# Gated linear attention and a gated feed-forward on one core: all five engine orders laid out anew

## The chip, the core and the metric

The kernel runs on one core of a Trainium2 chip. A core has five engines that run their own instruction lists side by side: TensorE (PE, matrix multiplies; the loads of its stationary operand stand as PEld), VectorE (DVE), ScalarE (ACT), GpSimd (POOL) and SyncE (SP, which here only issues DMAs). ACT and POOL issue DMAs too, each on a queue of its own. The engines wait for each other through semaphores. TensorE writes into eight PSUM banks, which VectorE and ScalarE empty. The metric is the device time of one execution in microseconds (us), lower is better.

## The reference

The first half is a gated linear attention over 4 batches, 8 heads, 768 tokens and 48 channels. The second half is a feed-forward block over the 3072 rows of the first one's result.

```python
f = 1.0 / (1.0 + np.exp(-f_logit))
for t in range(S):
    state = f[:, :, t, :, None] * state + np.einsum('bhd,bhe->bhde', k[:, :, t], v[:, :, t])
    y[:, :, t] = np.einsum('bhd,bhde->bhe', q[:, :, t], state)
...
gate = np.maximum(x @ w_gate, 0.0)      # x: (3072, 384), w_gate and w_val: (384, 1536)
val = x @ w_val
return (gate * val @ w_out)             # w_out: (1536, 384)
```

## The kernel before, in words

**Attention.** The recurrence is done in chunks of 128 tokens (6 chunks of 4 batches, 24 steps). For a step, ScalarE turns `f` into the logarithm of the gate (Exp, then Ln, lines 484 and 487, 768 columns for two steps at once). TensorE sums it along the tokens with a triangular matrix (names beginning with `cum`, lines 503 to 517), ScalarE takes Exp of the sum with both signs (lines 528 and 530) and of the chunk's total decay (line 538). VectorE or GpSimd multiply `q` and `k` with these (the "hats", names `hq` and `hk`, lines 552 on GpSimd and 553 on VectorE). The hats are transposed, on TensorE for the first eight steps (names `tq`, `tk`, line 564, and a copy to SBUF, names `cq`, `ck`, lines 568 and 569) and by a DMA for the others. Scores follow (`s`, lines 596 and 662), a mask on VectorE (`m`, lines 604 and 669), the result inside the chunk (`y`, lines 684 and 757), the part that comes from the state (`yi`, line 720) and the new state (`kv`, lines 707 and 784).

**Units.** The first eight steps are done as four units of two steps: unit 0 has the steps 00 and 01, unit 1 the steps 02 and 03, then 10 and 11, then 12 and 13 (a name such as `hk02` is the `k` hat of step 02). A unit works with pieces of the array: 64 matmuls of 64x32 for a `y`, 32 of 48x64 for its scores, 16 of 64x128 for a `kv`. Each of them is one matmul instruction and one weight load, so such a step issues many short instructions. These are the "tiled steps" below, with the scores (`s`) and the results (`y`) of later chunks that also use a part of the array.

**Feed-forward.** For a group of four steps (512 rows) and each of 12 blocks of 128 hidden columns, TensorE makes a gate (`g`) and a value (`u`), three matmuls each (line 804). ScalarE or VectorE applies the maximum with zero (`r`, lines 809 and 810), and VectorE multiplies (`p`, line 812). The first group's blocks 0 to 3 are done for two steps at a time (256 columns). The output projection (`o`, line 825) takes 12 matmuls a step, a copy (`d`) and a store. After some 20 us the feed-forward's matmuls fill TensorE between the attention's steps.

**What sets the order.** Nothing is scheduled at run time. A table `ORDER` lists, for each engine, the numbers of its operations in order; `BANKS` gives the PSUM bank of each result in the order in which TensorE opens them; `HELD` adds waits: `48: 10` lets operation 48 wait for operation 10. A negative number in TensorE's list stands for fill, matmuls on zeros (line 889) whose results are not used: `~3512` is three of 512 columns. Whoever opens a bank waits until its last tenant has been read. Semaphore waits follow from the data and these banks.

**Loads.** At the start each unit needs four transfers of 384 KB (`f`, `k`, `q`, `v`), written f0.0, k0.0 and so on for unit 0, f0.2 and so on for unit 1, f1.0 for the third, f1.2 for the fourth. They go over SP's queue, one (q0.0) over ScalarE's. The weights go over GpSimd's queue, in pieces.

## Time and profile before

| what | value |
|---|---|
| median of 3 runs | 193.1 us (192.79 to 193.47) |
| the profiled execution | 193.01 us, of it the span 191.3 us |
| TensorE busy | 180.6 us (94% of the span) |
| VectorE, ScalarE, GpSimd busy | 137.4 us, 92.0 us, 59.2 us |
| granted TensorE clock | 1.0 in all slices |

The span is the time from the first to the last instruction; 1.7 us of the profiled execution lie around it. A busy TensorE is not one at its peak, since matmuls overlap and their ends are modelled. So pauses are read from the starts of neighbouring instructions, and from the chain of work that ended last, which is followed back from the last instruction. "Issue" in a chain or a wait is time for which the profile names no reason. A name in a row such as L804 is the line of the kernel before; the lines of the changed kernel are one higher from the table on.

### The profile page before, as it was taken

The numbers are of one execution on the slowest core, as the hardware profiler recorded it, in microseconds if no ns is written. First come the engines' busy times: TensorE is split into PE (matmuls) and PEld (weight loads), VectorE is DVE, ScalarE is ACT, GpSimd is POOL, SyncE is SP. The second block draws the span as 40 slices with busy tenths as digits, with TensorE's granted clock in tenths as the row PEclk, the third lists the DMA queues.
The fourth block names the chain that finished last, engine by engine and source line by source line (L and its number), as shares of the span: only waits on it lengthen the run. The fifth ranks groups of instructions, "written<-read, shape, count | busy, mean of one in ns | idle before, by whom it ended". The sixth has DMA issues, their size and how long they took to land.

```text
span 191.3 us, 4793 instructions
## 1 busy us (share of the span) xinstructions
PE 180.6 (94%) x1977; PEld 108.4 (57%) x1996; DVE 137.4 (72%) x249; ACT 92.0 (48%) x200; POOL 59.2 (31%) x88
## 2 busy tenths in 40 slices
PE   7597999989899999999999999999999999999994
PEld 7364785455655556655555654556656554455562
DVE  4299877986758778669868779988688485655620
ACT  3969663264477546497654574372233132301112
POOL 5638531741036702047371610492600000000000
PEclk9999999999999999999999999999999999999999
DMA  6999999969999999989999999999763300000223
GB/s 163 318 296 216 159 209 264 161 123 251 225 221 206 240 201 246 235 191 200 197 182 215 245 175 175 243 251 178 98 151 108 99 4 0 3 0 0 109 98 126
DMA packets 110278, 32.43 MB, mean 170 GB/s; under 512 B 103472, under 2 KB 110000, under 8 KB 110256
## 3 DMA queue, kind: packets, MB, share of 16 engines
q1 hardware_dynamic: 88960, 25.04, 61.7%
q0 software_dynamic: 3744, 3.54, 12.2%
q10 hardware_dynamic: 17552, 3.54, 10.0%
q8 instruction: 16, 0.26, 0.6%
q14 instruction: 6, 0.05, 0.1%
HBM read 25.95 MB, written 4.72 MB: 160 GB/s over the span
## 4 chain that ended last, share of the span: by engine, by line
PE 85%; DVE 8%; DMA 3%; issue 2%; ACT 0%; DVEq 0%; ACTq 0%
PE ps L804 46%; PE ps L825 25%; DVE hats L553 4%; DMA q_in<-in_q_dram 3%; PE ps L596 2%; PE ps L757 2%; PE ps L564 2%; PE ps L514 1%; DVE gT L812 1%; PE ps L662 1%; PE ps L684 1%; PE ps L784 1%; DVE ptm L669 1%; PE ps L768 1%; PE ps L764 1%
## 5 line engine op out<-in xcount | busy, mean ns | idle before, releaser
L812 DVE TENSOR_TENSOR gT<-relu,ps 128x512 bf16<-128x512 bf16 (+1 forms) x76 | 47.7, 653 | 19.7 <-PE ps L804 17.5
L804 PE MATMUL ps<-xT,wv 128*128 128x512 bf16 (+1 forms) x220 | 53.6, 367 | 0.6 <-issue 0.2
L804 PE MATMUL ps<-xT,wg 128*128 128x512 bf16 (+1 forms) x219 | 52.6, 368 | 0.6
L825 PE MATMUL ps<-wo,gT 128*128 128x384 bf16 (+2 forms) x300 | 52.0, 320 | 0.0
L809 ACT ACTIVATE relu<-ps 128x512 bf16<-128x512 f32 (+1 forms) x42 | 23.9, 576 | 47.8 <-PE ps L804 24.2
L825 PEld LDWEIGHTS ps<-wo,gT 128*128 128x128 bf16 x300 | 27.7, 98 | 18.3
L804 PEld LDWEIGHTS ps<-xT,wg 128*128 128x128 bf16 x228 | 23.6, 108 | 20.5 <-issue 0.4
L804 PEld LDWEIGHTS ps<-xT,wv 128*128 128x128 bf16 x228 | 23.3, 108 | 18.3
L552 POOL TENSOR_TENSOR hats<-q_in,expo 128x384 bf16<-128x384 f32 x17 | 17.9, 1058 | 30.2 <-DMA q_in<-in_q_dram 12.2
L810 DVE TENSOR_SCALAR relu<-ps 128x512 bf16<-128x512 f32 (+1 forms) x34 | 21.7, 654 | 5.4 <-PE ps L804 5.3
L552 POOL TENSOR_TENSOR hats<-k_in,expo 128x384 bf16<-128x384 f32 x17 | 17.7, 1050 | 21.2 <-ACT expo L528 14.9
L604 DVE TENSOR_TENSOR ptm<-ps,tri 128x512 bf16<-128x512 f32 x32 | 20.5, 684 | 5.1 <-PE ps L596 5.1
L831 ACT ACTIVATE osb<-ps 128x384 f32<-128x384 f32 (+1 forms) x16 | 7.6, 484 | 25.0 <-PE ps L825 22.2
L528 ACT ACTIVATE expo<-ps 128x384 f32<-128x384 f32 x24 | 11.7, 496 | 6.1 <-DVE hats L553 2.6
L530 ACT ACTIVATE expo<-ps 128x384 f32<-128x384 f32 x24 | 11.8, 492 | 2.0 <-PE ps L517 1.9
L460 POOL TENSOR_TENSOR st<-ssum,dec 128x384 bf16<-128x384 f32 x10 | 8.6, 864 | 10.0 <-DVE ssum L458 10.0
L669 DVE TENSOR_TENSOR ptm<-ps,tmask 128x512 bf16<-128x512 f32 x16 | 10.0, 678 | 2.1 <-PE ps L662 2.1
L484 ACT ACTIVATE f_in<-f_in 128x768 f32<-128x768 f32 x12 | 10.1, 840 | 2.8 <-DMA f_in<-in_f_logit_dram 2.8
L458 DVE TENSOR_TENSOR ssum<-ps,st 128x384 f32<-128x384 f32 x16 | 8.8, 550 | 2.7 <-PE ps L784 2.5
L553 DVE TENSOR_TENSOR hats<-q_in,expo 128x384 bf16<-128x384 f32 x7 | 8.2, 1167 | 3.4 <-DMA q_in<-in_q_dram 3.4
L487 ACT ACTIVATE bneg<-f_in 128x768 bf16<-128x768 f32 x12 | 10.1, 841 | 1.0 <-ACT osb L831 0.8
L564 PE MATMUL ps<-ident,hats 128*128 128x128 bf16 x64 | 5.5, 220 | 4.0 <-DVE hats L553 3.0
(78 smaller groups left out, 159.2 us busy)
## 6 DMA issues: line engine op xcount, KB each, us to landing
v_in<-in_v_dram SPq DMA_DIRECT2D x12, 384.0 KB, 5.5
out_dram<-osb SPq DMA_DIRECT2D x23, 192.0 KB, 2.3
k_in<-in_k_dram SPq DMA_DIRECT2D x10, 384.0 KB, 7.1
q_in<-in_q_dram SPq DMA_DIRECT2D x9, 384.0 KB, 5.8
f_in<-in_f_logit_dram SPq DMA_DIRECT2D x8, 384.0 KB, 4.8
f_in<-in_f_logit_dram ACTq DMA_DIRECT2D x4, 384.0 KB, 6.6
q_in<-in_q_dram ACTq DMA_DIRECT2D x3, 384.0 KB, 5.6
wv<-in_moe_w_val_dram POOLq DMA_DIRECT2D x2, 384.0 KB, 6.7
```

The source lines that it names most:

```text
L484: add(f"ef{c}{b0}", by("ACT", lambda: sc.activation(raw, raw, AF.Exp, scale=-1.0), act_(n)), keys, keys, key=P)
L528: add(f"ek{c}{b}", by("ACT", lambda: sc.activation(ex[:, 1, :], bc.ap[:, 0:HD], AF.Exp, scale=1.0), act_(HD)), [bc], [f"expk{ei}"], key=P + 1)
L530: add(f"eq{c}{b}", by("ACT", lambda: sc.activation(ex[:, 0, :], bc.ap[:, 0:HD], AF.Exp, scale=-1.0), act_(HD)), [bc], [f"expq{ei}"], key=P ...
L552: return {**by("POOL", lambda: gp.tensor_tensor(o, i_, e_, ALU.mult), pool_(HD)), **by("DVE", lambda: ve.tensor_tensor(o, i_, e_, ALU.mult ...
L553: **by("DVE", lambda: ve.tensor_tensor(o, i_, e_, ALU.mult), dve_(HD))}
L604: add(f"m{c}{b}{j}", by("DVE", lambda b=b, j=j, mi=mi: ve.tensor_tensor(ptm[mi][:, j, :, :], s[b, j].ap[:, :].rearrange("p (n t) -> p n t" ...
L669: add(f"m{c}{b2[i]}{j}", by("DVE", lambda i=i, j=j, mask=mask: ve.tensor_tensor(ptm[mi[i]][:, j, :, :], s[j, i].ap[:, :].rearrange("p (n t ...
L804: z = te.matmul(bank.ap[:, 0:n], wt[:, kt, w_cols(j)], xT[xi][:, kt, n0:n1], start=(kt == 0), stop=(kt == NK - 1))
L809: add(f"r{c}{b0}.{j}", {**by("ACT", lambda: sc.activation(rdst, gate.ap[:, 0:n], AF.Relu), act_(n)), **by("DVE", lambda: ve.tensor_scalar_ ...
L810: **by("DVE", lambda: ve.tensor_scalar_max(rdst, gate.ap[:, 0:n], 0.0), dve_(n))}, [gate], [f"relu{ri}"], key=P)
L812: add(f"p{c}{b0}.{j}", by("DVE", lambda: ve.tensor_tensor(gT[gi][:, j, n0:n1], rdst, val.ap[:, 0:n], ALU.mult), dve_(n)), [val, f"relu{ri} ...
L825: z = te.matmul(o.ap[:, 0:e1 - e0], gT[gi][:, j, b * C:(b + 1) * C], wo[:, j, e0:e1], start=(j == 0), stop=(j == NJ - 1))
```

## The change

All numbers of the three tables change; the code below them stays. The operations are the same, but for the fill. Of the diff two lines of each kind tell it:

```diff
 ORDER = {
     "PE": [
-        45, ~60100, 74, 85, ~3512, 82, ~3512, 90, 80, 92, 121, ~1512, 95, 110, 101, 126, ~4512, 116, ~2512, 100, 128,
+        45, ~12512, 85, 74, ~9512, 110, 90, 121, 92, 82, 80, ~1512, 101, 95, 116, ~1512, 137, 126, 128, 118, 100, 104,
...
     "ACT": [
-        48, 72, 73, 108, 76, 75, 86, 87, 109, 84, 91, 122, 123, 111, 120, 127, 112, 77, 117, 113, 264, 103, 265, 228,
+        47, 49, 72, 73, 108, 76, 86, 75, 109, 87, 77, 113, 111, 122, 91, 93, 120, 123, 112, 130, 264, 117, 127, 129,
...
 HELD = {
-    48: 10, 57: 114, 60: 140, 67: 284, 69: 164, 70: 185,
+    47: 25, 56: 77,
 }
...
 BANKS = [
-    0, 1, 2, 3, 4, 5, 6, 7, 1, 2, 3, 4, 5, 6, 7, 1, 3, 7, 0, 2, 1, 4, 5, 6, 3, 0, 2, 7, 1, 5, 2, 0, 1, 3, 6, 0, 2, 3,
+    0, 1, 2, 3, 4, 5, 6, 7, 0, 1, 3, 7, 6, 5, 4, 0, 2, 6, 5, 7, 4, 6, 3, 0, 5, 7, 1, 4, 6, 0, 3, 4, 7, 6, 2, 5, 6, 7,
```

The fill goes from 60 matmuls of 100 columns and 13 of 512 to 24 of 512. Of the holds, those on q1.0 (60, after `yi03`), v1.2 (67), the weight loads wv2+2 (57), wv8+4 (69) and wo0+4 (70) go. New are one on k0.0 (47, after a memset of GpSimd) and one on the weight load wg2+2 (56), which now waits for ScalarE's decay of unit 0 (77, `dc00`). The places below are those that the prediction speaks of.

**The first loads.** SP's queue before, from its first row (f0.0 and f0.2, then k0.0, v0.0, k0.2, v0.2, q0.2, f1.2 and f1.0; q0.0 is ScalarE's first DMA):

```order
L408 DMA f_in<-in_f_logit_dram 128x8x96 x2
L408 DMA k_in<-in_k_dram 128x8x96
L408 DMA v_in<-in_v_dram 128x8x96
L408 DMA k_in<-in_k_dram 128x8x96
L408 DMA v_in<-in_v_dram 128x8x96
L408 DMA q_in<-in_q_dram 128x8x96
L408 DMA f_in<-in_f_logit_dram 128x8x96 x2
L408 DMA q_in<-in_q_dram 128x8x96 x2
```

SP's queue in the changed kernel, from the same place:

```order
L409 DMA f_in<-in_f_logit_dram 128x8x96 x2
L409 DMA q_in<-in_q_dram 128x8x96
L409 DMA k_in<-in_k_dram 128x8x96
L409 DMA v_in<-in_v_dram 128x8x96
L409 DMA q_in<-in_q_dram 128x8x96
L409 DMA f_in<-in_f_logit_dram 128x8x96 x2
L409 DMA q_in<-in_q_dram 128x8x96
L409 DMA k_in<-in_k_dram 128x8x96 x2
```

The q of unit 0 has come over to SP's queue, and k0.0 and v0.0 have gone to ScalarE's, where they are its first two instructions; what follows on SP stands one place further ahead.

**ScalarE around the Exp of f1.2.** Before, from the Exps of step 02 on (`expo<-ps4`; lines 528 and 530). The row of line 484 is the Exp of f1.2, the first row of line 487 its Ln; `qkT` are the copies of the transposes, `xT0<-ps3` is the first row block for the feed-forward:

```order
L528 ACTIVATE expo<-ps4 128x384
L584 ACTIVATE vpad2<-v_in 128x4x2x48
L569 ACTIVATE qkT<-ps7 128x512
L530 ACTIVATE expo<-ps4 128x384
L538 ACTIVATE dec<-ps0 64x4x2 x2
L569 ACTIVATE qkT<-ps1 128x512
L538 ACTIVATE dec<-ps4 64x4x2 x2
L484 ACTIVATE f_in<-f_in 128x768
L609 ACTIVATE xT0<-ps3 128x3x2x64
L487 ACTIVATE bneg<-f_in 128x16x48
```

In the changed kernel, from the last `v` copy of unit 1 on:

```order
L585 ACTIVATE vpad3<-v_in 128x4x2x48
L485 ACTIVATE f_in<-f_in 128x768
L570 ACTIVATE qkT<-ps4 128x512
L570 ACTIVATE qkT<-ps6 128x512
L570 ACTIVATE qkT<-ps5 128x512
L488 ACTIVATE bneg<-f_in 128x16x48
L610 ACTIVATE xT0<-ps4 128x3x2x64
L485 ACTIVATE f_in<-f_in 128x768
L488 ACTIVATE bneg<-f_in 128x16x48
```

The Exp of f1.2 now stands ahead of three copies of unit 1's transposes; before it stood behind the last of ScalarE's.

**VectorE in the first feed-forward group.** Before, from the last two 512-column maxima ahead of the first `hq` (step 11) to the end of the group's products:

```order
L810 TENSOR_SCALAR relu<-ps 128x512 x2
L812 TENSOR_TENSOR gT<-relu,ps 128x512 x2
L553 TENSOR_TENSOR hats<-q_in,expo 128x8x48
L812 TENSOR_TENSOR gT<-relu,ps 128x512 x2
L553 TENSOR_TENSOR hats<-k_in,expo 128x8x48
L810 TENSOR_SCALAR relu<-ps 128x512 x2
L553 TENSOR_TENSOR hats<-k_in,expo 128x8x48
L812 TENSOR_TENSOR gT<-relu,ps 128x512
L568 COPY qkT<-ps 128x512
L812 TENSOR_TENSOR gT<-relu,ps 128x512
```

In the changed kernel, from the hat of k for step 13 on:

```order
L554 TENSOR_TENSOR hats<-k_in,expo 128x8x48
L813 TENSOR_TENSOR gT<-relu,ps 128x512
L330 MEMSET dec 128x32
L813 TENSOR_TENSOR gT<-relu,ps 128x512
L811 TENSOR_SCALAR relu<-ps 128x512
L813 TENSOR_TENSOR gT<-relu,ps 128x512
L554 TENSOR_TENSOR hats<-q_in,expo 128x8x48
L813 TENSOR_TENSOR gT<-relu,ps 128x512
L569 COPY qkT<-ps 128x512
L811 TENSOR_SCALAR relu<-ps 128x512
L813 TENSOR_TENSOR gT<-relu,ps 128x512
L569 COPY qkT<-ps 128x512
```

Two hats stand among the 512-column operations where three stood (a hat of q, step 10, has moved ahead of them, between 256-column ones), and two copies of transposes are new there.

**TensorE's tiled steps of units 2 and 3.** Before, from the second scores on (line 662 scores, 707 `kv`, 684 `y`, 720 `yi`, 825 output projection, 514 and 517 sums):

```order
L662 MATMUL ps<-qkT 64x128 x32
L825 MATMUL ps<-wo,gT 128x384 x12
L707 MATMUL ps<-vpad,hats 128x96 x32
L684 MATMUL ps<-ptm,vpad 32x128 x128
L720 MATMUL ps<-qkT,st_0 32x128 x24
L514 MATMUL ps<-bneg,tri 128x384
L517 MATMUL ps<-ones,bneg 128x1 x4
L825 MATMUL ps<-wo,gT 128x384 x4
```

In the changed kernel, from the same scores on:

```order
L663 MATMUL ps<-qkT 64x128 x32
L826 MATMUL ps<-wo,gT 128x384 x12
L685 MATMUL ps<-ptm,vpad 32x128 x64
L708 MATMUL ps<-vpad,hats 128x96 x32
L826 MATMUL ps<-wo,gT 128x384 x8
L515 MATMUL ps<-bneg,tri 128x384
L518 MATMUL ps<-ones,bneg 128x1 x4
L826 MATMUL ps<-wo,gT 128x384 x4
L721 MATMUL ps<-qkT,st_0 32x128 x12
L685 MATMUL ps<-ptm,vpad 32x128 x64
L721 MATMUL ps<-qkT,st_0 32x128 x12
```

The two `y` steps, 64 matmuls each, stood back to back; now 12 matmuls of the output projection and a sum stand between them.

1 line of the change is left out of this document (added), and 98 rows, old and new, of tables (BANKS, ORDER).

## The prediction

> **What bounds the kernel now.** I read the page first, then the windows, TensorE's waits, the chain and, around each break in it, the timeline.
>
> ```profile
> PE 180.6 (94%) x1977; PEld 108.4 (57%) x1996; DVE 137.4 (72%) x249; ACT 92.0 (48%) x200; POOL 59.2 (31%) x88
> ...
> GB/s 163 318 296 216 159 209 264 161 123 251 225 221 206 240 201 246 235 191 200 197 182 215 245 175 175 243 251 178 98 151 108 99 4 0 3 0 0 109 98 126
> ...
> q8 instruction: 16, 0.26, 0.6%
> ```
> ```profile
> 76.34:81.20 4.86, 4.86 (x128) 3.27 (x128) 3.05 (x6) 2.33 (x9) 0.00 (x0) 1.00 1.27 234
> ```
>
> The first row holds busy time and instructions of each engine, the second the bytes moved in 40 slices of 4.8 us, the third the transfers of instructions. In the window's row the first column after its length is TensorE's busy time, with the count of matmuls: it is busy for the whole 4.86 us. The chain too runs along TensorE almost alone after the tiled steps of the first 60 us. So TensorE is the bound there, and since the change leaves its work as it is, time can only be won or lost in the first 60 us, at the end, and where TensorE changes its form of work. The chain names the places (start, length, work):
>
> ```profile
> 22.98 0.66 PE ps L684 x62
> ...
> 33.31 2.09 DVE hats L553
> 35.45 0.40 PE ps L564 x4
> ...
> 38.85 1.28 DVE hats L553
> 40.12 0.61 DVE gT L812
> 40.78 0.62 PE ps L564 x8
> ...
> 50.91 0.58 PE ps L684 x54
> 51.50 0.55 issue
> ...
> 167.16 0.65 PE ps L825 x4
> ```
>
> Three things are to be seen. Up to unit 1's `y` at 22.98 the start-up runs at the pace of loads, ScalarE and VectorE. Between 33 and 41 us VectorE's hats carry the chain. And at 51.5 us TensorE pauses inside a `y` step, after 54 of its 64 matmuls, where no semaphore is waited for.
>
> **The start.** In the changed kernel I follow ScalarE from the landing F of f1.2, since the Exp of f1.2 now stands ahead of three copies that unit 1 needs:
>
> ```profile
> 14.80 0.36 ACT L538 ACTIVATE dec<-ps 64x8 f32<-64x8 f32 x2
> ...
> 16.27 0.84 ACT L484 ACTIVATE f_in<-f_in 128x768 f32<-128x768 f32 x1
> 17.14 0.60 ACT L609 ACTIVATE xT<-ps 128x384 bf16<-128x384 f32 x1
> 17.60 0.82 ACT L487 ACTIVATE bneg<-f_in 128x768 bf16<-128x768 f32 x1
> 38.99 1.60 ACT L569 ACTIVATE qkT<-ps 128x512 bf16<-128x512 bf16 x3
> 25.59 0.89 ACT L528 ACTIVATE expo<-ps 128x384 f32<-128x384 f32 x2
> ```
> Exp 0.84, three copies 1.60, Ln 0.82, a row block 0.60, then Exp and Ln of f1.0, 0.84 and 0.82, make 5.5 us. The sums of units 2 and 3 then want four Exps and two decays before the bank of the last sum is free; two Exps take 0.89, a pair of decays 0.36, so 2.5 with two pairs. Unit 1's `y` follows at F + 8.0. It stands behind more work than before: three more 256-column matmuls and two sums of 384 columns. At the pace of the row at 167.16 (0.65 for four of 384 columns) that is 0.65. The old start of 22.98 is thus worth 23.6, and the start breaks even at F = 15.6.
>
> ```profile
> 4.15 1.15 SPq L408 DMA_DIRECT2D k_in<-in_k_dram  x1
> 5.35 2.69 SPq L408 DMA_DIRECT2D v_in<-in_v_dram  x1
> 5.75 0.93 POOL L435 DMA_DIRECT2D wg<-in_moe_w_gate_dram  x1
> ...
> 9.27 3.31 SPq L408 DMA_DIRECT2D f_in<-in_f_logit_dram  x2
> ```
> ```profile
> f_in<-in_f_logit_dram SPq DMA_DIRECT2D x1, 384.0 KB, 6.7
> ```
> ```profile
> k_in<-in_k_dram SPq DMA_DIRECT2D x1, 384.0 KB, 6.4
> v_in<-in_v_dram SPq DMA_DIRECT2D x1, 384.0 KB, 7.4
> wg<-in_moe_w_gate_dram POOLq DMA_DIRECT2D x1, 192.0 KB, 5.8
> ```
>
> The last number is the time from issue to landing. f1.2, issued at 9.27, landed at 15.97. The nine transfers up to it are the same after the change; which queue carries them shifts little, since in the second and third slice (4.8 to 14.3 us) the core already moves 318 and 296 GB/s. What differs is a weight slice of 192 KB (issued at 5.75, landed at 11.55), which now waits for unit 0's decay, near 9.7. It cost about 0.9: k0.2 landed at 10.55 and v0.2 2.2 later, where 384 KB at 300 GB/s take 1.3. So F is 15.1 if the slice stays behind f1.2, 16.0 if it comes in front again: a gain of 0.5 to a loss of 0.4. The cover of this gain is VectorE, which has a longer path to the same place now (two hats, a mask addition and a `v` copy ahead of unit 0's copies), and it can be held:
>
> ```profile
> 15.22 0.81 POOL L435 DMA_DIRECT2D wv<-in_moe_w_val_dram  x1 [1.54 <-DVE hats L553]
> 16.05 1.02 POOL L552 TENSOR_TENSOR hats<-q_in,expo 128x384 bf16<-128x384 f32 x1
> ```
> ```profile
> 14.36 0.55 DVE L553 TENSOR_TENSOR hats<-k_in,expo 128x384 bf16<-128x384 f32 x1
> 15.51 1.98 DVE L553 TENSOR_TENSOR hats<-q_in,expo 128x384 bf16<-128x384 f32 x1
> ```
>
> A hat takes 0.55 on VectorE with GpSimd idle, and 1.98 where GpSimd issues a load and then makes a hat. `hk00` meets such a run (the slice, a `v` copy, `hk02`) near 10 us. With 1.4 lost there, ScalarE's copies for unit 0 and the masks come later by as much, and `y` of unit 1 starts at 23.8 by VectorE's path, if F is not later than 15.8. I take that, +0.2 against 23.6, since that row is the nearest to what GpSimd does there; ends -1.1 (no hold, F at 14.5) and +1.0 (two holds, or F at 16.6).
>
> **The hats at 33 to 41 us.** The two hats of VectorE in the chain took 2.09 and 1.28 against 0.55, each beside a hat of GpSimd, and TensorE's transposes came late:
>
> ```profile
> 34.98 0.33 PE L503 MATMUL ps<-bneg,ident 128*128 128x384 bf16 x1
> 35.45 0.40 PE L564 MATMUL ps<-ident,hats 128*128 128x128 bf16 x4
> ```
> ```profile
> 39.36 0.61 PE L564 MATMUL ps<-ident,hats 128*128 128x128 bf16 x8
> 40.78 0.62 PE L564 MATMUL ps<-ident,hats 128*128 128x128 bf16 x8 [0.81 <-DVE gT L812]
> ```
>
> A 384-column matmul starts 0.16 before the next (0.65 for four), so the first pause is 0.47 - 0.16 = 0.3; eight transposes occupy 0.44 (four more take 0.62 - 0.40), so the second is 1.42 - 0.44 = 1.0. In the changed kernel one hat of q stands earlier, q1.0 and k1.0 are no longer held until 24 us, and GpSimd's hats come before the end of the group. Counted with 0.61 for a 512-column product (the chain at 40.12), VectorE reaches the end of the group's copies with some 2 us to spare, even if one hat loses 1.2 to GpSimd. Then -1.3; ends -1.6 (two small waits there go too) and 0 (they come back).
>
> **Blocks of instructions.** The q8 row shows 16 transfers of 16 KB for TensorE's 3973 matmuls and weight loads, about 250 instructions each. The pause at 51.5 ended a run that was short for that number, while the window shown first, with as many instructions, had none:
>
> ```profile
> 47.46:52.04 4.58, 4.04 (x131) 2.76 (x130) 3.64 (x7) 2.39 (x4) 0.00 (x0) 1.00 1.36 228
> ```
>
> I read it as TensorE waiting for its next block: about 260 instructions in 4.58 us with a pause of 0.55, 256 in 4.86 without. Counted on from there in blocks of 256, two blocks of the changed kernel come near 4.6. One reaches from unit 0's to unit 1's region of tiled steps, with some 5 us by the times above: +0.2, ends 0 and +1.2 (a fetch between busy weight loads may be slower). The other, with the separated `y` steps, has 4.1 of work against 3.9 before: its pause shrinks by 0.15, taken with the same uncertainty as 0.
>
> The Trainium skill (Runtime: NRT & Kernel Launch, Instruction fetch mechanics) says that blocks of 16 KiB, 256 instructions, are streamed and that crossing into one is "mostly hidden". By it both terms are nothing and the sum below is 0.2 lower. The pause in the middle of a step speaks against it.
>
> **Forms, and the end.**
>
> ```profile
> 47.17 0.33 PE L825 MATMUL ps<-wo,gT 128*128 128x384 bf16 x1
> 47.43 0.64 PE L662 MATMUL ps<-qkT 48*64 48x128 bf16 x32
> ...
> 187.55 0.49 ACT L831 ACTIVATE osb<-ps 128x384 f32<-128x384 f32 x1 [0.81 <-PE ps L825]
> ```
> From a full matmul to a tiled one it takes 0.26 instead of 0.16. Each change of tile form costs that 0.1; by the orders there are 41 before and 45 after: +0.4. The last step is now a full 384-column projection with a 192 KB store, where it was 256 columns and 128 KB: a third more in a copy of 0.49 is 0.16, and 64 KB at 300 GB/s are 0.2, in part beside each other: +0.2 (ends 0 and 0.4). The fill's new form changes nothing that I can see: the first one is sized to end where the Ln lands.
>
> **The sum.** 0.2 - 1.3 + 0.2 + 0.4 + 0.2 = -0.3 against the profiled execution's own 193.01, which lies 0.1 under the median: 192.7 us. All ends together (0.4 for the forms throughout) would reach from -2.3 to +3.0.
>
> **Rivals.**
> - *The start gains too.* No hold on VectorE, f1.2 at 14.5: 1.3 less than forecast, 191.4. For it: the slice of weights is out of the way. Against: GpSimd's run begins just when `hk00` is due.
> - *VectorE stays behind in the first group (slower).* GpSimd now has an unbroken run there (two weight issues, a hat, another issue, another hat, some 4.4 us by its rows), beside `hk13` and `hq13` on VectorE. One hold is covered; from some 2 us of lost time on TensorE's transposes wait again, and the 1.3 comes back: 194.0. For it: all three hats were held before. Against: the hats start earlier.
> - *The block inside unit 1's `y` comes late.* 1.0 more, 193.7. For it: the start packs more tiled steps into one block. Against: the elapsed time is over 4.6.
> - *TensorE's clock falls.* TensorE is sparse between 13 and 16.5 us, with two fill matmuls where there were six.
>
> ```profile
> 1.34:4.34 3.00, 3.00 (x37) 3.00 (x38) 1.21 (x13) 0.93 (x2) 1.69 (x11) 1.00 0.82 212
> ```
> At first 37 fill matmuls of 100 columns took 3.00, 81 ns each, where 100 columns at the later pace of 0.16 for 384 take 42: 3 us at the slow pace cost 1.5, with knock-on 2, so 194.7. None of the pauses quoted brought the slow pace back. The Trainium skill (TensorE: Matmul & The Clock Gate, Part 1) states a return to half clock after an idle window of about 3.4 us; no run here shows one.
>
> **Chances.** Forecast 0.41, early start 0.20, VectorE behind 0.22, late block 0.12, clock 0.05. A measurement of this kernel tells about 0.3% (0.6 us) from no change. The forecast's own range, 191.8 to 193.5, lies half on each side of 192.5, the bound of faster; the early start is faster; VectorE behind and the clock are slower; the late block falls half on each side of 193.7. So faster 0.41, same 0.26, slower 0.33. The range runs from 190.9 to 194.8: it takes in all rivals' times and leaves out the corners where several ends meet.
>
> **What would show it.** Right: unit 1's `y` (line 685) near 23.8; VectorE's two late hats of the first group at most once over 1 us and no TensorE pause above 0.3 before unit 3's scores; an issue pause of about 0.5 inside a `y` near 47 to 50; a last copy of 0.49. Wrong: a break in the chain after 60 us, where I found TensorE without a wait; an `issue` piece of 1 us in the first 25; or VectorE's hats as the chain's carriers again.

## The result, and the profile after

The changed kernel takes 194.9 us (median; 193.2 to 195.1) and the kernel before, run beside it, 193.5 (191.4 to 195.1). The ratio is 1.0069, with a 95% interval of 1.0047 to 1.0092: slower, on the other side of no change than forecast. Single executions of both kernels scatter by 2 to 4 us, so a single time says little here. Medians hold all executions, while the ratios leave out those more than 1.5% above their kernel's fastest, so a median and its ratio need not match. The two profiled executions, 193.01 and 194.41, differ by the same 1.4 us as the medians.

The chain of the changed kernel, in order of time (start, length, work):

```profile
1.32 5.71 DMA f_in<-in_f_logit_dram
7.05 0.84 ACT f_in L485
...
11.81 1.43 issue
...
13.98 2.35 DVE hats L554
16.33 0.47 DVE st L455
16.80 0.61 DVE ptm L670
17.41 0.81 PE ps L708 x16
...
25.91 0.57 PE ps L685 x52
26.48 0.49 issue
26.96 0.29 PE ps L685 x12
...
37.84 0.45 PE ps L565 x8
...
49.62 0.67 PE ps L685 x62
...
53.67 0.67 PE ps L685 x62
```

At the start there is more wait than before: the chain runs through the landing of f0.2 up to 7 us, then over VectorE, through 1.43 us that the chain calls issue (a `v` copy that is held, below) and one hat of 2.35 us, and unit 1's `y` begins at 25.91 where it began at 22.98. In that `y` TensorE now pauses after 52 of its 64 matmuls, with nothing named for it. Further on things are better: eight transposes at 37.84 go through in 0.45, without the pauses that stood at 35 and 40 us, and the two `y` steps near 50 us are whole.

How much each place is worth shows if from the start of an operation the work that TensorE did before it is taken off (three 512-column matmuls are 0.65, three of 256 columns 0.33, as in undisturbed rows; fill does not count as work). What is left is the time that TensorE lost up to there:

| lost up to | before | after | the step between |
|---|---|---|---|
| start of unit 1's `y` | 14.20 | 16.48 | +2.28 the start |
| end of its part from the state | 14.34 | 17.30 | +0.68 the pause in this `y` (0.49 as the chain counts it) |
| first output projection | 15.80 | 17.09 | -1.67 the hats at 33 to 41 us |
| sum of step 20 | 17.12 | 18.12 | -0.29: the pause of 0.55 is gone, and 0.26 is lost again, put down to more forms |
| last projection | 19.14 | 20.24 | +0.10 put down to forms |
| end | | | +0.3 the longer last copy and store |

The sum is +1.4. So the change won 2.2 us where TensorE waited for hats and for instructions, and lost 3.0 in the first 27 us.

The `v` copy in the kernel before, with GpSimd idle, and then what VectorE and GpSimd do at that place in the changed kernel (start, length, engine):

```profile
11.72 0.35 DVE L583 CAST vpad<-v_in 128x384 bf16<-128x384 f32 x1
```
```profile
11.78 1.54 DVE L584 CAST vpad<-v_in 128x384 bf16<-128x384 f32 x1
13.24 0.74 DVE L569 COPY qkT<-ps 128x512 bf16<-128x512 bf16 x2
13.90 2.43 DVE L554 TENSOR_TENSOR hats<-k_in,expo 128x384 bf16<-128x384 f32 x1
```
```profile
11.62 0.52 POOL L583 CAST vpad<-v_in 128x384 bf16<-128x384 f32 x1
12.09 1.00 POOL L553 TENSOR_TENSOR hats<-k_in,expo 128x384 bf16<-128x384 f32 x1
13.03 0.81 POOL L436 DMA_DIRECT2D wv<-in_moe_w_val_dram  x1
13.86 1.01 POOL L553 TENSOR_TENSOR hats<-q_in,expo 128x384 bf16<-128x384 f32 x1
```

A `v` copy that took 0.35 before takes 1.54, a hat that takes 0.55 takes 2.43: the copy beside a `v` copy and a hat of GpSimd, the hat beside two hats of GpSimd. The copies for unit 0's scores and the first mask stand behind them on VectorE, and TensorE, which has little to do meanwhile, loses its clock (the third column from the right in the windows):

```profile
12.00:14.00 2.00, 0.52 (x16) 0.40 (x16) 2.00 (x4) 2.00 (x6) 1.98 (x4) 1.00 1.17 324
14.00:16.00 2.00, 0.97 (x36) 0.71 (x36) 2.00 (x1) 1.64 (x3) 2.00 (x4) 0.90 1.32 244
16.00:18.00 2.00, 0.60 (x16) 0.71 (x17) 2.00 (x5) 0.00 (x0) 2.00 (x4) 0.50 1.29 254
...
20.00:22.00 2.00, 2.00 (x93) 1.44 (x72) 1.14 (x3) 1.90 (x4) 1.37 (x3) 0.50 1.38 219
```

Four things come together in the first 27 us, then: the landing of f0.2, the hold on VectorE, the clock, and the pause for instructions. The experiments take them one by one. Of the experiments each time is a median, and each ratio is to the kernel before run beside it (193.2 to 193.3).

### The profile page after: what moved, and what is told of

Its sections match the earlier page's. It is cut to its first block, busy times and chain, and to the rows that moved or that the text cites. A ratio compares the mean times of both kernels' runs of the same rounds, so it can differ in the third digit from the quotient of the medians.

```text
span 192.7 us, 4695 instructions
## 1 busy us (share of the span) xinstructions
PE 182.1 (95%) x1928; PEld 107.5 (56%) x1947; DVE 138.5 (72%) x254; ACT 91.1 (47%) x199; POOL 54.2 (28%) x84
## 4 chain that ended last, share of the span: by engine, by line
PE 85%; DVE 7%; DMA 3%; ACT 2%; issue 2%; SPq 0%; ACTq 0%
PE ps L805 45%; PE ps L826 24%; DMA f_in<-in_f_logit_dram 3%; PE ps L597 2%; PE ps L758 2%; DVE hats L554 2%; PE ps L565 2%; PE ps L685 2%; DVE gT L813 2%; PE ps L515 1%; DVE ptm L605 1%; PE ps L785 1%; PE ps L663 1%; PE ps L765 1%; PE ps L708 1%
## 5 line engine op out<-in xcount | busy, mean ns | idle before, releaser
L826 PE MATMUL ps<-wo,gT 128*128 128x384 bf16 (+2 forms) x300 | 53.1, 320 | 0.0
L810 ACT ACTIVATE relu<-ps 128x512 bf16<-128x512 f32 (+1 forms) x44 | 25.2, 588 | 50.1 <-PE ps L805 33.3
L826 PEld LDWEIGHTS ps<-wo,gT 128*128 128x128 bf16 x300 | 27.3, 98 | 17.6
L805 PEld LDWEIGHTS ps<-xT,wg 128*128 128x128 bf16 x228 | 23.8, 108 | 19.2
L811 DVE TENSOR_SCALAR relu<-ps 128x512 bf16<-128x512 f32 (+1 forms) x32 | 20.2, 636 | 7.3 <-PE ps L805 7.2
L553 POOL TENSOR_TENSOR hats<-q_in,expo 128x384 bf16<-128x384 f32 x13 | 13.0, 1001 | 17.7 <-ACT expo L531 16.5
L554 DVE TENSOR_TENSOR hats<-k_in,expo 128x384 bf16<-128x384 f32 x6 | 5.8, 970 | 5.3 <-ACT expo L529 5.3
L833 DVE COPY osb<-ps 128x384 f32<-128x384 f32 (+1 forms) x8 | 4.3, 534 | 7.4 <-PE ps L826 7.4
L583 POOL CAST vpad<-v_in 128x384 bf16<-128x384 f32 x8 | 4.0, 505 | 19.5 <-DMA v_in<-in_v_dram 19.5
```

Source lines behind the costliest of these rows:

```text
L553: return {**by("POOL", lambda: gp.tensor_tensor(o, i_, e_, ALU.mult), pool_(HD)), **by("DVE", lambda: ve.tensor_tensor(o, i_, e_, ALU.mult ...
L805: z = te.matmul(bank.ap[:, 0:n], wt[:, kt, w_cols(j)], xT[xi][:, kt, n0:n1], start=(kt == 0), stop=(kt == NK - 1))
L810: add(f"r{c}{b0}.{j}", {**by("ACT", lambda: sc.activation(rdst, gate.ap[:, 0:n], AF.Relu), act_(n)), **by("DVE", lambda: ve.tensor_scalar_ ...
L811: **by("DVE", lambda: ve.tensor_scalar_max(rdst, gate.ap[:, 0:n], 0.0), dve_(n))}, [gate], [f"relu{ri}"], key=P)
L826: z = te.matmul(o.ap[:, 0:e1 - e0], gT[gi][:, j, b * C:(b + 1) * C], wo[:, j, e0:e1], start=(j == 0), stop=(j == NJ - 1))
```

## Experiments on the first loads

**The first loads of before in the changed kernel.** In the lists 48 is q0.0, 47 and 49 are k0.0 and v0.0; 25, 15 and 38 are memsets, which only set when the first DMA of ScalarE goes out.

```diff
     "ACT": [
-        47, 49, 72, 73, 108, 76,
+        48, 72, 73, 108, 76,
...
     "SP": [
-        46, 50, 48, 53, 55,
+        46, 50, 47, 49, 53, 55,
...
-    47: 25, 56: 77,
+    48: 15, 56: 77,
```

> The changed kernel with the first loads on the queues of before: q0.0 on ScalarE's, k0.0 and v0.0 on SP's. Theory 1 (k0.0 and v0.0 on ScalarE's queue take bandwidth from f0.2, whose Exp stands on ScalarE ahead of the Exps of unit 0; it started at 7.05 instead of 5.85): the Exp of f0.2 starts near 5.9, the first hat at 7.6 to 7.9 instead of 8.69, unit 1's y up to 1.1 earlier, and the time is 193.8 to 194.4. Theory 2 (what is won ahead of VectorE's held copy and hat is lost in them again, since GpSimd's run starts when VectorE's does): the first hat is earlier, but y is not by more than 0.3, and the time stays within 0.3 of 194.9.

193.8 us, ratio 1.0022 (0.9986 to 1.0059): some 1.0 us under the changed kernel, and no longer to be told from the kernel before. The Exp of f0.2 in the kernel before, then ScalarE's, VectorE's and GpSimd's timelines in this run (the profiled execution took 192.85, 1.0 under the median):

```profile
5.85 0.83 ACT L484 ACTIVATE f_in<-f_in 128x768 f32<-128x768 f32 x1
```
```profile
6.00 0.83 ACT L485 ACTIVATE f_in<-f_in 128x768 f32<-128x768 f32 x1
```
```profile
11.48 0.29 DVE L584 CAST vpad<-v_in 128x384 bf16<-128x384 f32 x1
11.69 0.74 DVE L569 COPY qkT<-ps 128x512 bf16<-128x512 bf16 x2
12.35 1.15 DVE L554 TENSOR_TENSOR hats<-k_in,expo 128x384 bf16<-128x384 f32 x1
```
```profile
11.46 0.67 POOL L583 CAST vpad<-v_in 128x384 bf16<-128x384 f32 x1
```

The Exp of f0.2 is 1.05 earlier than in the changed kernel. The first hat is only 0.2 earlier, since it now waits for k0.0. Yet that small lead goes with a `v` copy of VectorE that is not held: it begins level with GpSimd's own `v` copy (11.48 and 11.46), where it began 0.16 behind it in the changed kernel (11.78 and 11.62). It takes 0.29, the hat behind it 1.15, and unit 1's `y` starts at 23.94, 1.9 earlier. Theory 1 has the time and the Exp right, but the first hat, at 8.48, missed its 7.6 to 7.9, and most of the price came by way of the hold, which theory 1 had not in it.

**The first loads of the changed kernel in the kernel before.**

```diff
     "ACT": [
-        48, 72, 73,
+        47, 49, 72, 73,
...
     "SP": [
-        46, 50, 47, 49, 53,
+        46, 50, 48, 53,
...
-    48: 10, 57: 114, 
+    47: 38, 57: 114, 
```

> The kernel before with k0.0 and v0.0 on ScalarE's queue and q0.0 on SP's, as in the changed kernel; nothing else moves. Theory 1 (this part of the change costs time by itself, through f0.2): the Exp of f0.2 starts at 7.0 to 7.4 instead of 5.85, and the time is 193.8 to 194.6, 0.6 to 1.4 over the kernel before. Theory 2 (it costs only through GpSimd's run in the changed orders): the Exp is as late, but unit 1's y moves by less than 0.4, and the time stays within 0.4.

195.2 us, ratio 1.0082 (1.0047 to 1.0117). Its chain:

```profile
1.33 6.40 DMA f_in<-in_f_logit_dram
7.72 0.02 issue
7.75 0.84 ACT f_in L484
...
24.00 0.67 PE ps L684 x62
```

The Exp of f0.2 starts at 7.75 instead of 5.85 and carries the chain, unit 1's `y` starts 1.0 later, and the time is 1.6 over that of the kernel before by the ratio. So these queues make the kernel slower by themselves, by more than theory 1 said. Two things in the run go beyond the change, though. With the other memset, k0.0 was issued at 0.98, not at 1.34 as in the changed kernel, and here the Exp of f0.0 came late too, at 5.13 (4.16 before, 4.19 in the changed kernel). And of the profiled execution's 1.9 us more only 0.4 were lost by the end of unit 2's `y`, where no pause for instructions stood; 1.5 were lost after 55 us, by waits that this experiment does not tie to f0.2. That the core moves more than 300 GB/s in both arrangements doesn't help: by these times k0.0 and v0.0 on a second queue share it with f0.2 instead of following it.

## Experiments on VectorE and GpSimd

**GpSimd's three hats to VectorE, all first weight slices behind them.** In the lists 114, 125 and 115 are hk02, hq03 and hq02; 56, 52 and 51 the slices wg2+2, wv0+2 and wg0+2.

```diff
     "DVE": [
-        84, 81, 83, 124, 102,
+        84, 81, 83, 114, 124, 125, 115, 102,
...
     "POOL": [
-        56, 94, 114, 52, 125, 40, 115, 51, 41, 57,
+        94, 40, 41, 56, 52, 51, 57,
...
-    47: 25, 56: 77,
+    47: 25, 56: 115,
```

> The changed kernel with GpSimd's work between 12 and 16 us taken away: the three hats hk02, hq03 and hq02 go to VectorE, and the first weight slices wait until hq02 is made. VectorE has three hats of 0.55 more, 1.65 us. Theory 1 (VectorE is held by GpSimd's hats and issues: 1.2 us in the v copy and 1.9 us in hk03): each of VectorE's hats takes 0.55 and the copy 0.35 to 0.5, the first mask of unit 0 is read at about 15.2 instead of 16.8, TensorE waits less, and the time is 193.0 to 193.8. Theory 2 (the operations are slow for themselves, or the longer order of TensorE sets y): the first mask comes at 17.5 or later and the time is 195 to 196.

195.4 us, ratio 1.0064 (1.0009 to 1.0119). The `v` copy took 0.29 and the hats 0.5 each, and the first mask came at 15.7, an us earlier with three hats more: the hold is gone as theory 1 says. But by the ratio the time is that of the changed kernel: it was lost again. TensorE waited 1.6 us for wg2+2, the slice that I had moved furthest. The next run keeps that slice at its place.

**The same with wg2+2 at its place.**

```diff
     "POOL": [
-        56, 94, 114, 52, 125, 40, 115, 51, 41, 57,
+        56, 94, 40, 41, 52, 51, 57,
...
-    47: 25, 56: 77,
+    47: 25, 56: 77, 52: 115,
```

> The changed kernel with the hats hk02, hq03 and hq02 on VectorE, and of the weight slices only the second and third held until hq02; the first slice, for which TensorE waited 1.6 us in the run with all slices held, keeps its place. Theory 1 (GpSimd's hats and issues hold VectorE, and this sets unit 1's y): the first mask of unit 0 is read at 15.7 instead of 16.7, no wait for a weight above 0.3 us stands ahead of y, y starts near 24.9 and the time is 193.8 to 194.4 if no pause for instructions grows. Theory 2 (the block of instructions sets the end of y, whatever VectorE does): y starts earlier and its pause grows by as much; its last matmul stays within 0.3 of 27.2, and the time within 0.3 of 194.9.

193.6 us, ratio 1.0012 (0.9977 to 1.0048): 1.1 to 1.2 us under the changed kernel. VectorE's timeline:

```profile
12.10 0.76 DVE L584 CAST vpad<-v_in 128x384 bf16<-128x384 f32 x1
12.78 0.73 DVE L569 COPY qkT<-ps 128x512 bf16<-128x512 bf16 x2
13.44 1.01 DVE L554 TENSOR_TENSOR hats<-k_in,expo 128x384 bf16<-128x384 f32 x2
14.37 1.01 DVE L554 TENSOR_TENSOR hats<-q_in,expo 128x384 bf16<-128x384 f32 x2
```

Four hats take 2.0 us where one took 2.43. Unit 1's `y` starts at 24.79 instead of 25.84. Theory 1 holds, though TensorE still waited 0.57 us for a weight slice ahead of `y`, where it allowed 0.3; theory 2 holds in part, since the pause in `y` grew by 0.2 and its last matmuls came 0.9 earlier, not 1.05. The Trainium skill (SBUF — State Buffer, Who interferes with whom) says that a VectorE instruction with two SBUF inputs contends with a GpSimd instruction that reads SBUF, and that one in a 2-port mode, which a cast can take, contends with GpSimd as well and is blocked where GpSimd began first. The rows agree: a hat took 0.5 with GpSimd making none, and 2.43 beside two.

**Both repairs of the start.** The edits of the kernel with the first loads of before and of the kernel just shown, together:

```diff
-    47: 25, 56: 77,
+    56: 77, 48: 15, 52: 115,
```

> The changed kernel with both repairs of its start: the first loads on the queues of before, and the hats hk02, hq03, hq02 on VectorE with the second and third weight slices held until hq02. Theory 1 (the two losses lie one behind the other): unit 1's y starts near 23.0 instead of 25.8 (23.9 with the queues alone, 24.8 with the hats alone); its pause grows to 1.3, since the transfer of instructions came 4 us after the block before it in every run of this order; the time is 192.4 to 193.0, 0.8 to 1.2 under the better of the two. Theory 2 (the two repairs remove the same loss, the hold on VectorE): y starts at 23.7 to 24.1, and the time is 193.3 to 193.8.

193.3 us, ratio 0.998 (0.9937 to 1.0024). `y` starts at 24.1 in the profiled execution; both are theory 2's values. So the two repairs seem to remove largely the same loss: an earlier VectorE escapes the hold, and a VectorE without a hold needs no lead. The intervals are too wide to tell the three runs apart (193.8, 193.6, 193.3). The pause did not grow to 1.3 there (it was 0.3 as the chain counts it). And `y` still starts 1.1 later than in the kernel before: what the rest of the new start costs was not taken apart.

**Unit 1's `y` behind two projections**, with both repairs (136 and 140 are `y` and its part from the state, 158 and 154 the projections):

```diff
-        241, 136, 140, 238, 158, 154,
+        241, 158, 154, 136, 140, 238,
```

> The kernel with both repairs, and in it unit 1's y and the part from the state behind the two 256-column values u00.3 and u00.2, six matmuls, instead of ahead of them. Theory 1 (TensorE only waits for its instructions there, so work of its own can fill that time): the pause in y shrinks by 0.6 to 0.9 and the time is 0.4 to 0.9 under that of the kernel with both repairs. Theory 2 (the copies of unit 1's rows, which follow y, are needed at once): the six matmuls are filled in, but TensorE waits as long behind y, and the time is the same within 0.2, or longer since u00.3 waits for its weights.

194.1 us, ratio 1.0055 (1.0004 to 1.0107). The pause in `y` is gone, and in its place TensorE waits 0.9 for a maximum ahead of the projections and 0.5 for the copy of unit 1's rows behind `y`. So theory 2 is right there, though TensorE waited for a maximum and not, as it said, for weights. The ten executions fall into two groups, 192.7 to 193.1 and 195.1 to 195.5; the profiled one, 192.8, is of the first, so what makes the second group longer isn't seen.

## Experiments on the clock

**More fill in the changed kernel where TensorE waits.** (101 is unit 0's first `kv`, 116 the transposes of hk02.)

```diff
-        80, ~1512, 101, 95, 116, ~1512, 137,
+        80, ~8512, 101, 95, ~10512, 116, ~1512, 137,
```

> The changed kernel with more fill on TensorE where it waits: eight matmuls of 512 columns instead of one ahead of unit 0's first kv, and ten ahead of the transposes of hk02. Nothing else moves. Theory 1 (the lower clock is a cost of its own): TensorE does too little between 12 and 17.5 us, the granted clock falls to half from about 15.5 to 22.8 us, and this costs 1.5 us. Then the clock stays at 1.0 here, unit 1's y starts near 24.4 instead of 25.8 and the time is 193.3 to 193.7. Theory 2 (the lower clock only accompanies a start that waits for VectorE): the clock stays at 1.0, but y starts at 25.3 or later, and the time is 194.4 to 195.0.

195.0 us, ratio 1.0074 (1.0038 to 1.011): no gain. The windows and the chain:

```profile
16.00:18.00 2.00, 2.00 (x27) 1.12 (x25) 2.00 (x4) 0.48 (x1) 2.00 (x5) 1.00 1.21 299
```
```profile
25.53 0.43 PE ps L685 x36
25.96 1.45 issue
27.40 0.40 PE ps L685 x28
```

The clock stays at 1.0 and `y` starts only 0.4 earlier, as theory 2 says. Then the pause is 1.45 instead of 0.49, and `y` ends 0.5 later than in the changed kernel, so the run leaves open what the clock alone costs. Note where it stands: 34 instructions more ahead of it, and it comes after 36 matmuls instead of 52.

**The same with both repairs**, where VectorE is no longer late:

```diff
-        80, ~1512, 101, 95, 116, ~1512, 137,
+        80, ~4512, 101, 95, ~7512, 116, ~1512, 137,
```

> The kernel with both repairs of the start, and more fill where TensorE still waits there: four matmuls of 512 columns instead of one ahead of unit 0's first kv, and seven ahead of the transposes of hk02. Theory 1 (the lower clock costs something of its own once VectorE is no longer late; of the ten executions of the kernel with both repairs the two at a clock of 1.0 took 191.97 and 192.12, the other eight 192.49 to 194.55): the clock stays at 1.0, the time is 191.9 to 192.5, below both kernels by more than 0.3%. Theory 2 (the lower clock costs nothing here either, since the transfer of instructions sets the end of unit 1's y): the clock stays at 1.0 and the time is 193.0 to 193.5, that of the kernel with both repairs.

193.2 us, ratio 0.9984 (0.9956 to 1.0013); with both repairs and without this fill it was 193.3, so theory 2 holds. The clock stays at 1.0, and the pause in `y` is 1.14 instead of 0.3. So neither run showed a price of the lower clock; in both the pause for instructions grew, which may have hidden it. The single executions don't settle it. Of the changed kernel's 20, the three at a clock of 0.998 or more took 193.2 to 193.6, against a median of 194.9. But with more fill all ten were at 0.998 or more, and nine of them took 194.7 to 195.1.

That TensorE's clock falls when it does little for some us is seen in the windows above: it was busy for 0.52 us of 12 to 14 and for 0.97 of 14 to 16, and within 14 to 24 us the granted clock was 0.5 for some 6.8 us. The Trainium skill (TensorE: Matmul & The Clock Gate, Part 1) puts the fall at an idle window of some 3.4 us, and by its figure the 6.8 us are two such windows. Here TensorE was not idle before it, but busy for a quarter to a half of the time.

## Experiments on the blocks of instructions

**The first fill of the kernel before with fewer instructions.**

```diff
-        45, ~60100, 74, 85,
+        45, ~12512, 74, 85,
```

> The kernel before with its first fill as 12 matmuls of 512 columns instead of 60 of 100: 48 matmuls and 48 weight loads fewer ahead of everything else. Theory 1 (the pause in unit 2's y is TensorE waiting for its next block of 256 instructions): the same block ends 96 instructions later in the program, so the pause of 0.55 stands 48 matmuls later, after about the 38th of the second y instead of the 54th of the first. Theory 2 (the pause has another cause at its place): it stays after the 54th. By both the time is within 0.4 of the kernel before.

198.6 us, ratio 1.016 (1.0037 to 1.0282). In its chain (the profiled execution is the longest of four, 201.4; it is used for the places, not for its time):

```profile
22.11 0.60 PE ps L684 x56
22.70 1.24 issue
23.94 0.25 PE ps L684 x8
```
```profile
51.44 1.01 PE ps L684 x96
52.45 5.15 issue
57.60 0.60 PE ps L684 x21
```

The pause left its place: where TensorE paused after the 54th of the 128 matmuls, it now does after about the 102nd (the chain misses some records; the timeline has 102), 48 matmuls later, as theory 1 says to the matmul. And a new one stands in unit 1's `y`. Wrong was the "within 0.4": 96 instructions fewer ahead of everything cost 3 us by the ratio. In this execution the pauses were 1.24 and 5.15, so a pause is not 0.55 wherever it falls; how long they were in the shorter executions (195.6, 197.2 and 200.0) no profile shows.

**The first fill of before in the changed kernel**, the same edit the other way:

```diff
-        45, ~12512, 85, 74,
+        45, ~60100, 85, 74,
```

> The changed kernel with its first fill as 60 matmuls of 100 columns, the form before, instead of 12 of 512: 96 instructions more ahead of everything, so each block of 256 instructions ends 48 matmuls earlier in the program. The block that ended after the 52nd matmul of unit 1's y (pause 0.66) then ends ahead of its 5th. Theory 1 (the pause is a transfer of instructions that comes late while data loads are under way; in five runs TensorE went on 1.35 to 1.68 us after its end): its block before ends near 18.0 us, the transfer comes 4 us later and lasts 0.9, so it is there by 24.5, before y starts at 25.8; the pause goes and the time is 194.0 to 194.4. Theory 2 (the y of unit 1 ends near 27.2 for reasons of data): the time stays within 0.3 of 194.9.

195.4 us, ratio 1.0113 (1.0077 to 1.0149). The pause moved ahead of the 5th matmul as said, but it did not go:

```profile
25.39 0.17 PE ps L685 x4
25.55 0.53 issue
26.08 0.70 PE ps L685 x58
```

The block before it ended at 19.9, not at 18.0: I had put its end at a wrong place in the order. Both theories missed the time. `y` ended 0.5 earlier, and 1.2 were lost at 149 us, where a copy waited for a store:

```profile
144.77 4.42 DMA out_dram<-osb
149.19 0.02 issue
149.21 0.50 ACT osb L832
```

**With the fill that keeps the clock as well**

```diff
-        45, ~12512, 85, 74, ~9512, 110, 90, 121, 92, 82, 80, ~1512, 101, 95, 116,
+        45, ~60100, 85, 74, ~9512, 110, 90, 121, 92, 82, 80, ~8512, 101, 95, ~10512, 116,
```

> Both: the first fill of 60 matmuls of 100 columns, and the fill that keeps the clock up (eight matmuls of 512 columns ahead of kv of unit 0, ten ahead of the transposes of hk02). Theory 1 (the lower clock costs something of its own, which a pause for instructions ate up in the run with fill alone): the clock stays at 1.0, unit 1's y starts near 25.4 and has no pause, and the time is 193.4 to 193.9, 0.4 to 0.7 under the kernel with the blocks moved alone. Theory 2 (the lower clock costs nothing here, since VectorE's copies and masks set the pace): the time is that of the kernel with the blocks moved alone, within 0.2.

it became 196.5 us, ratio 1.0195 (1.0129 to 1.0261). The block's end now lies ahead of `y`, among the projections at 23.2, where TensorE waits 2.8 us. That is in the longest of the four executions, 198.7, whose clock then fell (0.981 over the span); the other three kept 1.0 and took 195.9 to 196.7. Both theories fall, and the most fill gave the longest of the three.

What these pauses have in common comes from the trace's own records of the 16 KB transfers, with TensorE's instructions counted in blocks of 256 and the count set by the one pause of the kernel before. A transfer that starts after the end of one block brings the block that TensorE needs at the end of the next; "goes on" is that later end. In the row of the first loads of before TensorE waits at the block's end from 17.4 on; the table has the end of that wait:

| kernel | a block ends | the next transfer starts | it ends | TensorE goes on |
|---|---|---|---|---|
| before, third `y` | 47.46 | 49.09 | 50.36 | 52.04 |
| before, unit 1's `y` | 16.14 | 17.73 | 19.32 | no wait (22.94) |
| after | 20.96 | 24.73 | 25.61 | 26.96 |
| more fill | 20.53 | 25.04 | 25.96 | 27.40 |
| first loads of before | 18.75 | 23.04 | 23.92 | 25.40 |
| both repairs | 19.07 | 22.64 | 23.61 | 25.06 |
| both repairs and fill | 18.81 | 23.63 | 24.55 | 25.99 |
| before with less fill, fourth `y` | 50.69 | 54.73 | 56.04 | 57.60 |

Where TensorE waited it goes on 1.35 to 1.7 us after the transfer's end, each time (1.26 and 1.29 in two runs that are not in the table). The transfer takes 0.9 to 1.6. What varies is its start: 1.6 to 4.8 us after the block's end in these rows, and in the same traces up to 2.3 us ahead of it where less is loaded. In the kernel before, for instance, a transfer starts at 117.26 for a block that ends near 118.5, with the DMA engines' share at 0.82, against 1.20 to 1.38 from 20 to 26 us in the changed kernel.

That the pauses belong to blocks of 256 can be counted more closely. TensorE's waits for semaphores are instructions too (13 up to that pause in the changed kernel). With them, the twelve pauses of this kind in the profiled executions of eleven kernels stand after TensorE's instruction 704 (ten of them, all near unit 1's `y`) or 1472 (the kernel before, and with less fill), to the instruction. Both are three quarters of a block over whole blocks, and they are three blocks apart. So where TensorE waited, passing a block of 256 instructions took 4.6 to 7.2 us, and 256 instructions of tiled steps with some projections are, by the same rows, 4 to 5.5 us of work.

**Nearly all weights held until unit 1's `y` is done** (140 is its part from the state):

```diff
     "POOL": [
-        51, 41, 57, 62, 63, 106, 3, 68,
+        51, 41, 106, 3, 57, 62, 63, 68,
...
-    47: 25, 56: 77,
+    47: 25, 56: 77, 57: 140,
```

> The changed kernel with the weight loads from wv2+2 on held until unit 1's y and the part from the state are done; TensorE then has to wait for them, so the whole gets longer, 197 or more, and only the transfers of instructions ahead of that are looked at. Theory 1 (a transfer of instructions waits behind GpSimd's weight loads; where much of these was under way, it began 3.4 to 4.8 us after the end of the block before, elsewhere 0.1 to 2.7): with less of them between 20 and 25 us it begins at most 2.7 us after the block's end, instead of 3.8, and the pause in y shrinks from 0.66 to under 0.2. Theory 2 (the 4 us are the same whatever loads): it begins 3.5 to 4.5 us after, and the pause stays.

201.6 us, longer as expected. The transfer starts 2.65 us after the block's end instead of 3.76, as theory 1 says, and `y`, which also starts 0.7 later, has no pause:

```profile
26.53 0.74 PE L685 MATMUL ps<-ptm,vpad 64*32 64x128 bf16 x64
```

**Only wg4+4 and wv4+4 later** (62 and 63; 106 is sd10, 107 the copy x01):

```diff
     "POOL": [
-        57, 62, 63, 106, 3, 68,
+        57, 106, 62, 63, 3, 68,
...
-    47: 25, 56: 77,
+    47: 25, 56: 77, 62: 107,
```

> The changed kernel with two weight loads later, and nothing else moved: wg4+4 and wv4+4 (384 KB each) wait for the copy x01 of unit 0's rows on VectorE, and stand behind sd10 on GpSimd, so they are issued at about 22 instead of 17.5 us. TensorE needs them from 29.9 us on. Theory 1 (the transfer of instructions for unit 1's y waits behind weight loads issued ahead of it; with nearly all weights held it began 2.65 us after the end of the block before, instead of 3.76, and the pause was gone): it begins 1.5 to 2.7 us after, the pause in y falls from 0.66 to under 0.2, and the time is 194.2 to 194.5 if the weights are there in time. Theory 2 (it waits behind all loads alike, and SP's fill the gap): it begins 3.4 us or more after, the pause stays, and the time is 194.7 to 195.1.

194.7 us, ratio 1.0055 (1.0023 to 1.0087). The transfer starts 4.0 us after the block's end: theory 1 falls for these two loads, and the time is theory 2's. The pause is gone in the profiled execution only because `y` starts at 27.3, after a longer stretch at half clock. **With both repairs of the start**

```diff
-    56: 77, 48: 15, 52: 115,
+    56: 77, 48: 15, 52: 115, 62: 107,
```

> The kernel with both repairs of the start, and these two weight loads as late. Theory 1: the transfer begins at most 2.7 us after the block's end (3.6 without), the pause in unit 1's y falls from 0.5 to nothing in the profiled execution, and from 1.3 where the clock stays up; the time is 192.2 to 192.8, 0.3 to 0.5% below the kernel before. Theory 2: the transfer begins as late, and the time is 193.0 to 193.5; or the weights come late for the 512-column projections, and a wait for wg of 0.5 or more stands at 27 to 30 us.

it is 192.7 us, ratio 0.9986 (0.9954 to 1.0018), the lowest median of all, but not to be told from the kernel before. The transfer starts 3.6 us after the block's end, as without the edit, and the pause is 0.8: theory 2 for the transfer, though the time is one that theory 1 gave. What delays the transfers is thus open. Less load at that time went with an earlier start in one run, but the two loads that I suspected are not it.

## An experiment that failed

**The orders of before up to unit 1's `y`, then those of the changed kernel.**

```diff
     "PE": [
...
-        136, 140, 144, 241, 146, 150, 174, 172,
+        136, 140, 144, 150, 146, 277, 241, 238,
...
-    48: 10, 57: 114, 60: 140, 67: 284, 69: 164, 70: 185,
+    48: 10, 57: 114,
```

> The orders of the kernel before up to unit 1's y, and from there on the orders of the changed kernel. Theory 1 (the change loses at the start only, and the gain on the hats at 33 to 41 us stands on its own): y starts at 22.9 to 23.3, the pauses of 0.3 and 1.0 us between 33 and 41 us are gone, and the time is 191.7 to 192.6, below both kernels. Theory 2 (the hats are on time only because the changed start gives them 2.9 us more): the pauses come back, and the time is 193.2 to 194.0.

198.1 us, ratio 1.0244 (1.016 to 1.0329). Neither theory is tested by it. With the hold on q1.0 gone, the loads of units 2 and 3 went out ahead of the weights, and TensorE waited for these, as the list of its waits from 20 to 42 us shows:

```profile
PE ps L805 <- DMA wg<-in_moe_w_gate_dram: 2.0, 1, 2.0
PE ps L805 <- ACT xT L610: 1.1, 1, 1.1
PE ps L805 <- DVE gT L813: 0.4, 1, 0.4
```

So the hold of the kernel before, which looked like a hindrance for the hats, seems to have guarded the first weights. The pauses between 33 and 41 us were gone in this run, as theory 1 said, but the start is not comparable. The gain on the hats rests on the accounting of the two profiled executions; no run isolates it.

## Why the prediction was wrong

The forecast was 192.7 with a range to 194.8; the kernel takes 194.9, and the sign was wrong. By its terms:

- **The start, +0.2 forecast, +2.3 measured.** This is the step that failed. "Which queue carries them shifts little, since the core already moves 318 and 296 GB/s" is wrong: the order of landing matters, not the sum, and the Exp of f0.2 came 1.2 us later. The two runs on the first loads give +1.6 and -1.1 us for it, the first with f0.0 late as well. And the hold on VectorE was taken once, at `hk00`, for 1.4. `hk00` took 0.55, at 10.72, beside a weight issue of GpSimd alone; the hold came later and twice, at the `v` copy (1.2) and at hk03 (1.9). "Two holds" stood as the upper end of the term, +1.0, priced without the late start that brings VectorE into GpSimd's run. F, the landing of f1.2 on which I built the first half of the term, was earlier than 14.3 and set nothing. As the text said, VectorE's path decides then; only its length was wrong.
- **The hats at 33 to 41 us, -1.3 forecast, -1.67 measured.** Right, and at the end that includes the small waits. VectorE's two late hats took 1.18 and 0.55 (rows at 34.05 and 38.43 of its timeline), one over 1 us, as forecast. The rival in which VectorE stays behind there did not come.
- **The blocks of instructions, +0.2 and 0 forecast, +0.68 and -0.55 measured.** Pauses stand where blocks of 256 end; the count was right in every kernel above that has such a pause. What was wrong is the model of a fixed 4.6 us for a block. Passing a block took 6.0 us in unit 1's `y`, and 4.06 without any pause near 50 us, since there the transfer started 0.7 us after the block's end and not 1.6. The -0.55 I counted as nothing; the spread-out `y` steps did get through. The "mostly hidden" of the Trainium skill (Runtime: NRT & Kernel Launch, Instruction fetch mechanics) is right for most blocks of these traces. It is wrong by 0.3 to 5 us for those that the tiled steps fill.
- **The forms, +0.4, and the end, +0.2.** From the first output projection to the last projection the changed kernel lost 0.36 more apart from the pause of 0.55, and 0.3 at the end. That is near the forecast, but no run shows that the 0.36 are the changes of form.
- **The clock.** It fell, as the rival with a chance of 0.05 has it, at about its place, and the text's "none of the pauses quoted brought the slow pace back" was a reason too weak for so low a chance: the pauses here were longer. But its price of 2 us is not shown: keeping the clock changed the time by nothing in two kernels, with a longer pause for instructions in both.
- **The signs.** What was to show it right, `y` near 23.8, failed at once, and no pause stood in a `y` near 47 to 50. Of those that were to show it wrong, "an issue piece of 1 us in the first 25" came: 1.43 at 11.81, the held `v` copy on VectorE, besides TensorE's 0.49 at 26.48. The chain also leaves TensorE after 60 us, for VectorE from 118.3 to 121.9 and from 151.4 to 155.1, but the list of TensorE's waits from 60 us on is empty, so no time was lost by it.

So the gains that were forecast came, at the hats and, beyond the forecast, near 50 us where the tiled steps are spread: 2.2 us. The start, with the pause in unit 1's `y`, took 3.0 back. Of that the old queues for the first loads return 1.1, the hats taken from GpSimd 1.2, and both 1.6, by the medians.

## What to carry to other kernels

Bandwidth that is full says nothing on which transfer lands first; before moving a load to another queue, ask which landing the first chain waits for, and what then shares the bandwidth with it. A loss at one place can have two sufficient causes: either repair of the start won 1.1 or 1.2 us, both together 1.6. And in a kernel of many short TensorE instructions, count them in blocks of 256: an edit that only adds or drops fill moves every block's end, and can cost more than what it was meant to mend.

## What was unexpected of the hardware

TensorE stood inside a run of ready matmuls, waiting for instructions: for 0.3 to 1.5 us in most of these runs, and for 5.15 in an execution 2.8 us over its kernel's median. The next block's transfer starts up to 4.8 us after a block's end while much data is loaded, and up to 2.3 ahead of it where less is; TensorE goes on 1.3 to 1.7 us after the transfer's end. What holds the transfer back was not found: later weight loads of 384 KB each did not bring it forward.

A start of VectorE's `v` copy level with GpSimd's own, or 0.16 us behind it, went with 0.29 and 1.54 us for the same copy.
